# Zero matmuls planned into TensorE's gaps at the start of an attention and FFN kernel, with changes to an eviction's engine, a load step and the last stores

## The chip, the cores and the metric

The kernel runs on one core of a Trainium2 chip. The metric is the device time of one execution in microseconds; lower is better. Five engines share the work: TensorE (PE), VectorE (DVE), ScalarE (ACT), GpSimd (POOL) and SyncE (SP), which here only issues DMAs.

## The reference

Memory attention for 8 batches of 8 heads, then a feed-forward layer over the 4,608 tokens:

```python
a = softmax(phi, axis=2)                       # batch, head, token, 32 memories
k_m, v_m = a^T k, a^T v                        # per batch and head: 32 x 64
attn = softmax(q k_m^T / 8, axis=-1)           # token x 32
x = concat_heads(attn v_m)                     # 4608 x 512
h = x @ w_in                                   # 512 x 2048
g = h * erf(softplus(h))
out = g @ w_out                                # 2048 x 512
```

Inputs and output are float32; `w_in` and `w_out` arrive as float64 words and are decoded on the chip.

## The kernel before

**Work.** For one batch `memories` computes the memories' weights (exponential of phi), then `k_m` and `v_m` by the 40 small matmuls of `one_memory` (L504, called kvmv below), evicts them (`kvk`, L514 and L516), turns them with two transposes (L521) and writes `km` and `vm` (L534, L537). `attention` multiplies q by `km` (L547), and DVE and ACT make the softmax of it: transpose (L593), maximum, subtract, exponential on ACT (L601), sum, reciprocal, product (L607) and a transpose back into `at` (L614). `vw` multiplies `w_in` by `vm` (also L547), so that the first FFN product is `psh = vw x at` (`ffn1`, L645) and x is never formed.

**Steps.** A step is one of 16 blocks of 128 FFN columns of one batch; there are 128. Per step `ffn1` makes two halves of 288 tokens in PSUM, DVE copies each into `h` (L655), ACT makes softplus (L662, from `h` into `e`) and erf (L667), DVE multiplies `e` and `h` into `g` (L679 in the first batch, L686 later), and `ffn2` multiplies `g` by `w_out` into the accumulators `pso0` to `pso3` (L712), four column blocks a step, six steps after `ffn1` (`LAG`). The 64 tokens that remain per batch go two batches at a time into `psr`. In the first batch (steps 0 to 15) `ffn2` uses float32 operands, later pairs of float32r parts (`g_hi`, `g_lo`); `ffn1` changes to pairs at step 4. Softplus, erf and exponential need different ACT tables, so steps run in groups of four: four softplus, then four erf.

**Weights.** Each of the 8 blocks of `w_in` and of `w_out` is 1 MB. `decode` turns one into float32 with a clamp (L393), a merge (L407) and a sign instruction (L429) on DVE and two instructions on ACT (L399, L403).

**Order.** Class `Plan` records every operation with an engine, a cost in ns, a rank (100 per step, some ahead of or behind it), its reads and writes. `Plan.order` then builds the order by a simulation: at each turn, of what can start soonest on each engine, the operation with the lowest rank; the instructions are issued in just that order, and semaphores do the rest. Buffers count too: pool `raw` holds 4 tiles for phi, kv and q, `wo` 8 for weights, `ot` 2 for results, `el` 5 of `h` and 5 of `e`, `ps` 4 PSUM banks.

**Start and end.** 12 matmuls of zeros (`warm`, L326) open TensorE's work. The first loads are issued in a fixed order: phiT, phi, two kv, the first `w_in`, two kv, two q, then weights. The loads and the memory work of the second batch are entered 14 steps ahead of its first step (L814). At the end `store` (L750) evicts each accumulator with one ACT instruction of 128x512 into a tile of pool `ot` (L753), and SP sends it out (L755).

Of the kernel before, what the change touches and what calls it, by code (L numbers as in the profile page):

```python
# [42 lines left out]
class Op:  # L43
    def __init__(self, engine, cost, rank, emit, kind, nbytes, edge):
        self.engine, self.cost, self.rank, self.emit = engine, cost, rank, emit
        self.kind, self.nbytes, self.edge = kind, nbytes, edge
        self.before, self.after, self.tiles, self.placed = set(), [], set(), []
        self.ready = self.start = self.end = 0.0


class Plan:
# [6 lines left out]
    RELOAD = 100.0  # L58
    NEAR = 100.0

    def __init__(self, room, any_order):
# [9 lines left out]

    def op(self, engine, cost, rank, reads, writes, emit, kind=None, nbytes=0, edge=None, after=(), holds=()):
        x = Op(engine, cost, rank, emit, kind, nbytes, edge)
        x.before.update(after)
# [30 lines left out]
    def order(self):  # L105
# [10 lines left out]
        landed, warm_at, pe_end = 2200.0, 4000.0, 0.0  # L116
        releases, out, now, held = [], [], 0.0, set()

        def fits(x):
# [8 lines left out]
            return all(room[p] >= n for p, n in need.items())  # L128

        while len(out) < len(self.ops):  # L130
            best = None
            for e, xs in waiting.items():
                can = [x for x in xs if fits(x)]
                if e == ACT and not at_edge:
                    can = [x for x in can if x.kind != "exp"]
                if not can:
                    continue
                t0 = max(free[e], now, min(x.ready for x in can))
                can = [x for x in can if x.ready <= t0 + self.NEAR]
                if e == PE and small and any(x.kind == "small" and x.ready <= t0 for x in can):  # L140
                    can = [x for x in can if x.kind == "small" and x.ready <= t0]
                x = min(can, key=lambda x: x.rank)
                t = max(free[e], x.ready, now)
                if best is None or t < best[0]:
                    best = (t, x)
            if releases and (best is None or releases[0][0] <= best[0]):
# [3 lines left out]
            if best is None:  # L150
                raise RuntimeError(f"nothing fits after {len(out)} of {len(self.ops)}")
            now, x = best
            e = x.engine
            waiting[e].remove(x)
# [5 lines left out]
            cost, late = x.cost, 0.0  # L160
            if e == PE:
                if now - pe_end > 3400:
                    warm_at = now + 4000
                if now < warm_at:
                    cost *= 2
                if (x.kind == "small") != small:
                    small = not small
                    cost += self.SWITCH if small else self.SWITCH + self.RELOAD
                pe_end, late = now + cost, 170.0
            elif e == ACT:  # L170
                if x.kind is not None and x.kind != table:
                    cost += self.TABLE
                    table = x.kind
                if x.edge is not None:
                    at_edge = x.edge
                late = 75.0
            elif e == DVE:
                late = 60.0
            free[e] = now + cost
            x.start, x.end = now, now + cost + late  # L180
# [5 lines left out]
            for y in x.after:  # L186
                n_wait[y] -= 1
                y.ready = max(y.ready, x.end + self.SIGNAL)
                if not n_wait[y]:
                    waiting[y.engine].append(y)  # L190
            for k in x.tiles:
# [9 lines left out]
def tile_memory_attention_then_erf_softplus_ffn(  # L201
# [11 lines left out]
    P = 128  # L213
# [22 lines left out]
    FR1, FR2 = 4, 16  # L236
    WARM = (12, 12, 16)

# [82 lines left out]

    def warm(n, rank, after):
        def emit():
            t = pools["ps"].tile([P, DM], F32, name="warm", tag="ps")
            for _ in range(n):
                nc.tensor.matmul(out=t, lhsT=zeros[:, :P], rhs=zeros, start=True, stop=True)  # L326

        key = plan.tile("ps", "warm", n, rank)
        return op(PE, 216 * n, rank, [("zeros",)], [key], emit, after=after)

# [299 lines left out]
    def ffn1(rank, i, half):  # L630
# [10 lines left out]
        def emit():  # L641
# [74 lines left out]
    def ffn2(rank, i, d):  # L716
# [11 lines left out]

        op(PE, mm(DM, True) if exact else 3 * mm(DM, False), rank, gs + [w_key, o], [o], emit)
        if k == NK - 1:  # L730
# [19 lines left out]
    def store(rank, o, rows):  # L750
        t = tile_("ot", "ot", *o)
        op(ACT, on_act(DM, True), rank - 30, [o], [t],
           lambda: nc.scalar.activation(get(t), get(o), AF.Identity))  # L753
        for n, (r, ln) in enumerate(rows):
            op(SP, 60, rank, [t], [], lambda n=n, r=r, ln=ln: nc.sync.dma_start(  # L755
                out=out[r : r + ln], in_=get(t)[n * ln : (n + 1) * ln]), nbytes=ln * DM * 4)

# [12 lines left out]

    for g in range(NG):
        load_phiT(-2000, 0, g)
    load_phi(-1999, 0)
    load_kv(-1998, 0, 0)
    load_kv(-1997, 0, 1)
    load_weight(-1996, "in", 0)
    load_kv(-1995, 0, 2)
    load_kv(-1994, 0, 3, "wo")
    load_q(-1993, 0, "wo")
    load_q(-1992, 1, "wo")  # L780
    load_weight(-1991, "in", 1)
    load_weight(-1990, "out", 0)
    for c in range(2, NPR):
# [3 lines left out]

    w = [warm(WARM[0], -3000, ())]
    memories(at(-10), at(-9), 0)
# [10 lines left out]
    for c in range(NPR):  # L800
        if c:
            when(2 * c - 3, decode, at(2 * c - 3), "in", c)
            when(2 * c - 1, vw, at(2 * c - 1.5), 0, c, 1, 2 * c < FR1)
        when(2 * c, decode, at(second[2 * c] - 3.5), "out", c)
        n = second[16 + 2 * c] - 5 - c
        when(n, split_wo, at(n), c)
# [89 lines left out]
```

## Time and profile before

| | |
|---|---|
| median of 3 runs | 739.71 us (738.8 to 740.99) |
| the profiled execution's own time | 740.94 us |
| its span, first to last instruction | 739.2 us |
| TensorE busy | 710.2 us, 96% of the span |
| VectorE busy | 524.4 us, 71% |
| ScalarE busy | 446.5 us, 60% |
| GpSimd busy | 100.5 us, 14% |
| mean granted TensorE clock | 0.972 of full speed |

The busy share of an engine is an average over the span. In the strip of 40 slices (18.5 us each) TensorE shows 6, 5, 6 tenths in the first three, 9 or more from there to the last but one, and 6 in the last; its granted clock is 7, 5, 8 and 8 tenths in the first four slices and full after. DMA is at 9, 9, 9 and 6 tenths in the first four.

### The profile page before, as it was taken

How to read it: one execution, taken by the hardware profiler on the slowest of the kernel's cores; microseconds unless marked ns; L12 is line 12 of the kernel's file. 1: busy time of each engine (PE TensorE's matmuls, PEld its weight loads, DVE VectorE, ACT ScalarE, POOL GpSimd, SP SyncE). 2: the span in 40 equal slices, each digit the busy share in tenths (PEclk: the TensorE clock that was granted, in tenths of full speed). 3: DMA queues.
4: the chain of work that ended last, by engine and by line, in shares of the span. 5: the costliest groups of instructions: out<-in, count | busy, mean ns of one | idle time of the engine just before them, and what ended most of it. 6: DMA issues, size and time to landing. Idle time of an engine off the chain costs nothing.

```text
span 739.2 us, 12098 instructions
## 1 busy us (share of the span) xinstructions
PE 710.2 (96%) x4716; PEld 550.2 (74%) x4716; DVE 524.4 (71%) x975; ACT 446.5 (60%) x691; POOL 100.5 (14%) x246
## 2 busy tenths in 40 slices
PE   6569999999999999999999999999999999999996
PEld 3246555668788887888788887888878788888885
DVE  3898998879875687777755496777754587666730
ACT  4698887776776566585753457574654266454611
POOL 0001111110111011111111011111111111111110
PEclk7588999999999999999999999999999999999999
DMA  9996313162331224211130212311210100010002
GB/s 307 379 385 212 114 58 128 38 213 81 94 117 32 90 63 124 86 58 33 65 97 1 90 47 73 120 44 47 65 33 1 58 15 1 1 51 7 1 1 71
DMA packets 30392, 64.74 MB, mean 88 GB/s; under 512 B 2688, under 2 KB 13440, under 8 KB 29312
## 3 DMA queue, kind: packets, MB, share of 16 engines
q1 hardware_dynamic: 30336, 63.97, 26.0%
q8 instruction: 37, 0.61, 0.3%
q14 instruction: 19, 0.16, 0.1%
HBM read 54.53 MB, written 9.44 MB: 87 GB/s over the span
## 4 chain that ended last, share of the span: by engine, by line
PE 91%; DMA 6%; ACT 1%; SPq 1%; DVE 0%; issue 0%; ACTq 0%
PE pso L712 50%; PE psh L645 27%; PE psr L712 6%; PE psa L547 5%; DMA kv<-kv 2%; PE psa L504 2%; DMA phiT<-phiT 2%; DMA q<-qT 1%; DMA out<-ot 1%; PE psa L521 0%; ACT w L403 0%; SPq L346 0%; ACT ot L753 0%; SPq L359 0%; SPq L361 0%
## 5 line engine op out<-in xcount | busy, mean ns | idle before, releaser
L712 PE MATMUL pso<-wo,g_hi 128*128 128x512 f32 x896 | 281.1, 395 | 0.0
L662 ACT ACTIVATE e<-h 128x576 f32<-128x576 f32 x128 | 87.7, 685 | 176.0 <-DVE h L655 175.6
L712 PEld LDWEIGHTS pso<-wo,g_hi 128*128 128x128 f32 x896 | 159.9, 188 | 32.4 <-issue 6.8
L712 PE MATMUL pso<-wo,g_lo 128*128 128x512 f32 x448 | 176.0, 393 | 0.0
L655 DVE COPY h<-psh 128x288 f32<-128x288 f32 x256 | 114.7, 451 | 42.1 <-PE psh L645 40.1
L645 PE MATMUL psh<-at_hi,vw_hi 128*128 128x288 f32 x496 | 114.1, 311 | 0.0
L645 PEld LDWEIGHTS psh<-at_hi,vw_hi 128*128 128x128 f32 x496 | 84.6, 189 | 29.6 <-issue 8.6
L645 PE MATMUL psh<-at_lo,vw_hi 128*128 128x288 f32 x496 | 106.4, 296 | 0.0
L645 PE MATMUL psh<-at_hi,vw_lo 128*128 128x288 f32 x496 | 106.0, 295 | 0.0
L686 DVE TENSOR_TENSOR e<-e,h 128x576 f32<-128x576 f32 x112 | 82.9, 751 | 29.3 <-ACT e L667 29.2
L693 POOL CAST rest<-g_hi 128x64 fp32r<-128x64 f32 x112 | 50.5, 452 | 388.2 <-DVE g_hi L688 379.8
L712 PEld LDWEIGHTS pso<-wo,g_lo 128*128 128x128 f32 x448 | 84.1, 188 | 19.3
L688 DVE CAST g_hi<-e 128x576 fp32r<-128x576 f32 x112 | 50.9, 457 | 64.1 <-PE pso L712 52.1
L689 DVE TENSOR_TENSOR g_lo<-e,g_hi 128x576 fp32r<-128x576 f32 x112 | 86.3, 771 | 5.4 <-PE pso L712 0.6
L667 ACT ACTIVATE e<-e 128x576 f32<-128x576 f32 x128 | 80.6, 676 | 0.4
L645 PEld LDWEIGHTS psh<-at_hi,vw_lo 128*128 128x128 f32 x496 | 80.1, 189 | 0.0
L645 PEld LDWEIGHTS psh<-at_lo,vw_hi 128*128 128x128 f32 x496 | 79.3, 188 | 0.0
L712 PE MATMUL pso<-w,g 128*128 128x512 f32 x112 | 53.4, 612 | 0.0
L693 POOL CAST rest<-g_lo 128x64 fp32r<-128x64 f32 x112 | 36.6, 327 | 109.6 <-DVE g_lo L689 101.8
L712 PE MATMUL psr<-wo,rest 128*128 128x512 f32 x192 | 49.0, 390 | 0.0
L317 ACT ACTIVATE vw_hi<-psa 128x512 fp32r<-128x512 f32 (+1 forms) x68 | 35.3, 554 | 22.1 <-PE psa L547 22.0
L319 DVE TENSOR_TENSOR vw_lo<-psa,vw_hi 128x512 fp32r<-128x512 f32 (+1 forms) x68 | 41.7, 632 | 6.8 <-ACT vw_hi L317 6.7
(79 smaller groups left out, 692.1 us busy)
## 6 DMA issues: line engine op xcount, KB each, us to landing
kv<-kv SPq DMA_DIRECT2D x32, 512.0 KB, 5.0
q<-qT SPq DMA_DIRECT2D x16, 576.0 KB, 5.2
w<-w_in SPq DMA_DIRECT2D x8, 1024.0 KB, 11.1
w<-w_out SPq DMA_DIRECT2D x8, 1024.0 KB, 11.3
out<-ot SPq DMA_DIRECT2D x32, 256.0 KB, 2.1
phiT<-phiT SPq DMA_DIRECT2D x16, 288.0 KB, 3.1
phi<-phi SPq DMA_DIRECT2D x8, 512.0 KB, 5.7
kv<-kv SPq DMA_DIRECT2D x32, 64.0 KB, 4.9
```

The lines of the kernel that those rows point to most:

```text
L317: lambda: nc.scalar.activation(get_hi(), get_src(), AF.Identity))
L319: lambda: nc.vector.tensor_tensor(out=get_lo(), in0=get_src(), in1=get_hi().bitcast(F32), op=ALU.subtract))
L547: nc.tensor.matmul(out=get(ps[par])[p * M : (p + 1) * M, :], lhsT=w()[rows, p, :], rhs=x()[rows, p, :], start=True, stop=True,)
L645: nc.tensor.matmul(out=get(ps), lhsT=x[:, g, k % 4 * P : (k % 4 + 1) * P], rhs=y[:, g, :], start=(n + g == 0), stop=(n == len(parts) - 1 a ...
L655: op(DVE, on_dve(U), rank - 20, [ps], [(h, half)], lambda: nc.vector.tensor_copy(out=get(h)[:, half * U : (half + 1) * U], in_=get(ps)))
L662: last[:] = [op(ACT, on_act(S), rank, [("h", i)], [e], lambda: nc.scalar.activation(get(e), get(("h", i)), AF.Softplus), kind="softplus", ...
L667: last[:] = [op(ACT, on_act(S), rank, [e], [e], lambda: nc.scalar.activation(get(e), get(e), AF.Erf), kind="erf", edge=edge, after=last)]
L686: op(DVE, on_dve(S), rank, [e, h], [e], lambda: nc.vector.tensor_tensor(out=get(e), in0=get(e), in1=get(h), op=ALU.mult))
L688: op(DVE, on_dve(S, 1), rank, [e], [hi], lambda: nc.vector.tensor_copy(out=get(hi), in_=get(e)))
L689: op(DVE, on_dve(S), rank, [e, hi], [lo], lambda: nc.vector.tensor_tensor(out=get(lo), in0=get(e), in1=get(hi).bitcast(F32), op=ALU.subtract))
L693: lambda x=x, y=y: nc.gpsimd.tensor_copy(out=rest[:, k, x, cols], in_=get(y)[:, NT * P :]))
L712: nc.tensor.matmul(out=o, lhsT=y, rhs=z, start=(start and n == 0), stop=(stop and n == len(parts) - 1))
```

## The change

- `warm` is gone. Instead the planner notes a number `fill` for a TensorE operation that starts more than 450 ns after the one before it: gap less 200 ns, divided by 216 ns or, where the planner's picture of the clock is low, 432 ns. That many zero matmuls (128x512, bfloat16, into a bank of its own that later becomes `pso0`) are issued ahead of the operation. This ends with the first `ffn2` of a batch (kind "stop filling"). The groups, in order: 14, 12, 3, 15, 3, 2, 2, 35, 8, 11, 4, 3, in all 112, where before there were 12.
- The copy of `psh` into `h` may go to DVE or ACT for steps 0 to 15, whichever the planner finds free sooner. In the built program ACT has 17 of these 32, DVE 15.
- The second batch's loads and memory work are entered 12 steps ahead (`o - 12`) instead of 14.
- `store`: for the last batch and its `psr`, the tile comes from tag `h` (5 buffers) instead of `ot` (2), and the eviction is two instructions of 256 columns, one on ACT, one on DVE.
- Without effect on the built program: `AHEAD` is 0, so the new branch that uses it is never taken; the first loads are written as a list in the same order; the other value for `split_wo` applies at `2 * c >= 16`, which does not occur.

```diff
+class Clock:
[...]
...
-        waiting = {e: [x for x in self.ops if x.engine == e and not n_wait[x]] for e in ENGINES}
+        waiting = {e: [x for x in self.ops if e in x.ways and not n_wait[x]] for e in ENGINES}
...
+        def best_way(x):
+            return min(x.ways, key=lambda e: max(free[e], x.ready, now) + x.ways[e][0])
...
             if e == PE:
-                if now - pe_end > 3400:
-                    warm_at = now + 4000
-                if now < warm_at:
-                    cost *= 2
+                filling = filling and x.kind != "stop filling"
+                gap = now - max(free[PE], 1100.0)
+                if filling and gap > 450:
+                    x.fill = int((gap - 200) / (216 if clock.fast else 432))
+                    clock.to(now, 1.0)
+                else:
+                    clock.to(now, 0.0)
...
+                if not clock.fast:
+                    cost *= 2
...
-    WARM = (12, 12, 16)
+    H_EITHER = 16
...
+    def fill(n):
+        if n and not idle:
+            idle.append(pools["po"].tile([P, DM], F32, name="idle", tag="pso0"))
+        for _ in range(n):
+            nc.tensor.matmul(out=idle[0], lhsT=zeros[:, :P], rhs=zeros, start=True, stop=True)
...
-        op(DVE, on_dve(U), rank - 20, [ps], [(h, half)], lambda: nc.vector.tensor_copy(
-            out=get(h)[:, half * U : (half + 1) * U], in_=get(ps)))
+        op(DVE, on_dve(U), rank - 20, [ps], [(h, half)],
+           lambda: nc.vector.tensor_copy(out=keep(), in_=get(ps)),
+           other={ACT: (on_act(U, True), lambda: nc.scalar.activation(keep(), get(ps), AF.Identity))}
+           if i < H_EITHER else ())
...
-        t = tile_("ot", "ot", *o)
-        op(ACT, on_act(DM, True), rank - 30, [o], [t],
-           lambda: nc.scalar.activation(get(t), get(o), AF.Identity))
+        final = o[1] >= B - 2 if o[0] == "psr" else o[1] == B - 1
+        t = tile_("h" if final else "ot", "ot", *o)
+        halves = [(0, DM // 2, ACT), (DM // 2, DM, DVE)] if final else [(0, DM, ACT)]
...
-        n = o - 14 if b == 1 else max(o - 21, NK - 2)
+        n = o - 12 if b == 1 else max(o - 21, NK - 2)
...
+        fill(x.fill)
         x.emit()
```

The planner's new costs move instructions on every engine in the first batch. Three places follow.

**VectorE, the last rows up to the first product `g`** (`h` copies, `at_lo` and `vw_lo` are float32r remainders, `pmx`, `psm`, `prs`, `phi` belong to the second batch's memory, `w` rows are decodes). Before:

```order
L407 SCALAR_TENSOR_TENSOR w<-w 128x1024
L393 TENSOR_SCALAR w<-w 128x1024
L487 TENSOR_SCALAR psm<-psm 128x1
L429 SCALAR_TENSOR_TENSOR w<-w 128x1024
L487 TENSOR_SCALAR psm<-psm 128x1
L489 RECIPROCAL prs<-psm 128x1 x2
L655 COPY h<-psh 128x288 x2
L393 TENSOR_SCALAR w<-w 128x1024
L407 SCALAR_TENSOR_TENSOR w<-w 128x1024
L393 TENSOR_SCALAR w<-w 128x1024
L429 SCALAR_TENSOR_TENSOR w_in_104<-w 128x4x256
L679 TENSOR_TENSOR g<-e,h 128x576
```

Now:

```order
L443 SCALAR_TENSOR_TENSOR w<-w 128x1024
L356 TENSOR_TENSOR vw_lo<-psa,vw_hi 128x256
L465 SCALAR_TENSOR_TENSOR w<-w 128x1024
L356 TENSOR_TENSOR vw_lo<-psa,vw_hi 128x256
L443 SCALAR_TENSOR_TENSOR w<-w 128x1024
L696 COPY h<-psh 128x288
L465 SCALAR_TENSOR_TENSOR w_in_104<-w 128x4x256
L493 TENSOR_SCALAR pmx<-pmx 128x1 x2
L429 TENSOR_SCALAR w<-w 128x1024
L721 TENSOR_TENSOR g<-e,h 128x576
```

Between the transposes into `at` and the first `g` stand, now as before, 4 merges, 4 sign instructions, two `at_lo`, two `vw_lo` and two maxima; gone from there are 6 of 10 `h` copies, 1 of 5 clamps, and the second memory's `phi` (two instructions), `psm` and `prs` (two each). On ACT the four erf of steps 0 to 3 now stand ahead of the second memory's exponentials, not behind them.

**TensorE, around the first `ffn2`.** Before:

```order
L504 MATMUL psa<-kv,phi 32x128 x20
L547 MATMUL psa<-w_in_104,vm_101 32x256 x8
L645 MATMUL psh<-at_hi,vw_hi 128x288 x2
L645 MATMUL psh<-at_lo,vw_hi 128x288 x2
L645 MATMUL psh<-at_hi,vw_lo 128x288 x2
L712 MATMUL pso<-w,g 128x512 x3
```

Now (the fill row is the last of three; ahead of the three stands `psa<-w_in_104,vm_101`):

```order
L365 MATMUL idle<-zeros 128x512
L501 MATMUL psa<-ident,bias 128x128 x2
L681 MATMUL psh<-at_hi,vw_hi 128x288 x2
L681 MATMUL psh<-at_lo,vw_hi 128x288 x2
L681 MATMUL psh<-at_hi,vw_lo 128x288 x2
L754 MATMUL pso<-w,g 128x512 x2
L681 MATMUL psh<-at_hi,vw_hi 128x288 x2
L681 MATMUL psh<-at_lo,vw_hi 128x288 x2
L681 MATMUL psh<-at_hi,vw_lo 128x288 x2
L754 MATMUL pso<-w,g 128x512 x2
L540 MATMUL psa<-kv,phi 32x128 x20
```

The second batch's first kvmv (20 rows here, 40 in the trace, where a float32 matmul is two) stood ahead of the first `ffn2` and now stands behind its four.

**TensorE, the third batch's second kvmv and its first q product** (`psa<-q,km_99`). Before:

```order
L504 MATMUL psa<-kv,phi 32x128 x20
L712 MATMUL pso<-wf,g 128x512 x2
L521 MATMUL psa<-ident,kvk 128x128 x2
L645 MATMUL psh<-at_hi,vw_hi 128x288 x2
L645 MATMUL psh<-at_lo,vw_hi 128x288 x2
L645 MATMUL psh<-at_hi,vw_lo 128x288 x2
L645 MATMUL psh<-at_hi,vw_hi 128x288 x2
L645 MATMUL psh<-at_lo,vw_hi 128x288 x2
L645 MATMUL psh<-at_hi,vw_lo 128x288 x2
L547 MATMUL psa<-q,km_99 32x288 x8
```

Now, the last rows ahead of that product; the kvmv stands eight rows further up, with two `ffn1` halves and the transposes between:

```order
L754 MATMUL pso<-w,g 128x512 x4
L681 MATMUL psh<-at_hi,vw_hi 128x288 x2
L681 MATMUL psh<-at_lo,vw_hi 128x288 x2
L681 MATMUL psh<-at_hi,vw_lo 128x288 x2
L681 MATMUL psh<-at_hi,vw_hi 128x288 x2
L681 MATMUL psh<-at_lo,vw_hi 128x288 x2
L681 MATMUL psh<-at_hi,vw_lo 128x288 x2
L754 MATMUL pso<-wf,g 128x512 x4
L583 MATMUL psa<-w_in_105,vm_102 32x512 x8
L583 MATMUL psa<-q,km_99 32x288 x8
```

On SP the rows agree up to the fourth `w_in` load; after it two of the second batch's kv loads stand ahead of the next `w_out`. GpSimd's rows change place with the products they copy from.

## Rows read from the trace of the kernel before

**Rows 1.** Windows, TensorE alone: length, busy us (instructions), granted clock, DMA share, GB/s.

```profile
0.00:9.00 9.00, 5.36 (x14) 1.00 0.81 275
9.00:37.00 28.00, 17.15 (x158) 0.51 1.04 366
37.00:49.00 12.00, 8.62 (x54) 1.00 1.03 374
49.00:61.00 12.00, 9.13 (x69) 0.57 1.04 381
61.00:732.00 671.00, 669.30 (x4423) 1.00 0.20 63
```

**Rows 2.** Timeline of the first 61 us, TensorE: start, us, what, idle before and releaser.

```profile
16.82 2.50 PE L504 MATMUL psa<-kv,phi 128*32 128x128 f32 x36 [1.18 <-DMA kv<-kv]
19.87 0.76 PE L521 MATMUL psa<-ident,kvk 128*128 128x128 f32 x2 [0.55 <-ACT kvk L514]
20.57 2.85 PE L547 MATMUL psa<-q,km 64*32 64x288 f32 x32
31.54 4.18 PE L645 MATMUL psh<-at,vw_hi 128*128 128x288 f32 x8 [7.04 <-DVE at L614]
56.91 4.38 PE L712 MATMUL pso<-w,g 128*128 128x512 f32 x6
61.92 0.42 PE L645 MATMUL psh<-at_hi,vw_hi 128*128 128x288 f32 x2
```

**Rows 3.** The same timeline, the weight loads of two neighbouring zero matmuls.

```profile
1.59 0.15 PEld L326 LDWEIGHTS <-zeros 128*128 128x128 bf16 x1 [0.27 <-issue]
2.02 0.15 PEld L326 LDWEIGHTS <-zeros 128*128 128x128 bf16 x1 [0.28 <-issue]
```

**Rows 4.** Timeline after 61 us, TensorE: the same work at the higher clock.

```profile
63.51 0.38 PE L521 MATMUL psa<-ident,kvk 128*128 128x128 f32 x2
64.69 1.43 PE L504 MATMUL psa<-kv,phi 128*32 128x128 f32 x40
67.04 0.66 PE L547 MATMUL psa<-w_in,vm 64*32 64x256 f32 x16
73.85 0.72 PE L547 MATMUL psa<-q,km 64*32 64x288 f32 x16
127.08 1.88 PE L712 MATMUL pso<-w,g 128*128 128x512 f32 x4
```

**Rows 5.** Chain of waits in order of time: start, us, engine, tile, line.

```profile
80.57 3.43 PE pso L712 x8
159.66 1.58 PE psh L645 x12
```

**Rows 6.** Timeline, VectorE: start and end of its first chain, and two later products.

```profile
22.50 1.81 DVE L593 STREAM_TRANSPOSE sc<-psa 128x288 f32<-128x288 f32 x4 [2.95 <-PE psa L547]
30.62 1.43 DVE L614 STREAM_TRANSPOSE at<-sc 128x576 f32<-128x576 f32 x2
54.03 0.75 DVE L679 TENSOR_TENSOR g<-e,h 128x576 f32<-128x576 f32 x1
124.08 1.42 DVE L679 TENSOR_TENSOR g<-e,h 128x576 f32<-128x576 f32 x2
```

**Rows 7.** Groups of instructions, shapes apart: count, busy us, mean ns, idle before.

```profile
L655 DVE COPY h<-psh 128x288 f32<-128x288 f32 x256 | 114.7, 451 | 42.1 <-PE psh L645 40.1
L393 DVE TENSOR_SCALAR w<-w 128x1024 f32<-128x1024 f32 x16 | 11.0, 685 | 4.4 <-DMA w<-w_in 4.4
L572 ACT ACTIVATE vw_hi<-psa 128x256 f32<-128x256 f32 x4 | 1.3, 382 | 2.2 <-PE psa L547 2.2
```

**Rows 8.** Windows, all engines: length, PE, PEld, DVE, ACT, POOL busy, clock, DMA share, GB/s.

```profile
65.00:70.00 5.00, 5.00 (x70) 3.35 (x62) 5.00 (x9) 4.96 (x12) 0.00 (x0) 1.00 0.58 182
100.00:140.00 40.00, 40.00 (x216) 23.70 (x201) 36.55 (x63) 28.32 (x41) 5.50 (x7) 1.00 0.19 60
```

**Rows 9.** Timeline, ScalarE: the second memory's exponentials, first and last instruction.

```profile
45.85 1.28 ACT L485 ACT_TABLE_LOAD   x1
49.63 0.40 ACT L480 ACTIVATE phi<-phi 64x256 f32<-64x256 f32 x1
```

**Rows 10.** Timeline, third batch's first q product: its load and the product.

```profile
151.85 0.93 SPq L376 DMA_DIRECT2D q<-qT  x2
157.24 0.84 PE L547 MATMUL psa<-q,km 64*32 64x288 f32 x16 [1.70 <-DMA q<-qT]
```

**Rows 11.** Timeline of the end: last matmuls and evictions.

```profile
731.14 1.52 PE L712 MATMUL psr<-wo,rest 128*128 128x512 f32 x6
732.04 1.28 ACT L753 ACTIVATE ot<-pso 128x512 f32<-128x512 f32 x2 [1.48 <-DMA out<-ot]
734.82 0.60 ACT L753 ACTIVATE ot<-psr 128x512 f32<-128x512 f32 x1 [1.49 <-DMA out<-ot]
```

More of the change, by code (lines that the diff above doesn't have):

```diff
@@ L70, in tile, with op @@
         return key
-    def op(self, engine, cost, rank, reads, writes, emit, kind=None, nbytes=0, edge=None, after=(), holds=()):
-        x = Op(engine, cost, rank, emit, kind, nbytes, edge)
+    def op(self, engine, cost, rank, reads, writes, emit, kind=None, nbytes=0, edge=None, after=(),
+           holds=(), other=()):
+        x = Op({engine: (cost, emit), **dict(other)}, rank, kind, nbytes, edge)
         x.before.update(after)
@@ L135, in order @@
                     can = [x for x in can if x.kind != "exp"]
+                can = [x for x in can if len(x.ways) == 1 or best_way(x) == e]
                 if not can:
@@ L138, in order @@
                 t0 = max(free[e], now, min(x.ready for x in can))
[L139 to L142, printed above, removed]
+                near = [x for x in can if x.ready <= t0 + self.NEAR]
+                if e == PE and small and any(x.kind == "small" and x.ready <= t0 for x in near):
+                    near = [x for x in near if x.kind == "small" and x.ready <= t0]
+                elif e in (ACT, DVE) and self.AHEAD:
+                    near = [x for x in can if x.ready <= t0 + self.AHEAD]
+                    near = [min(near, key=lambda x: x.rank + self.WORTH * max(0.0, x.ready - t0))]
+                x = min(near, key=lambda x: x.rank)
                 t = max(free[e], x.ready, now)
                 if best is None or t < best[0]:
-                    best = (t, x)
+                    best = (t, x, e)
             if releases and (best is None or releases[0][0] <= best[0]):
@@ L151, in order @@
                 raise RuntimeError(f"nothing fits after {len(out)} of {len(self.ops)}")
-            now, x = best
-            e = x.engine
-            waiting[e].remove(x)
+            now, x, e = best
+            x.engine, (cost, x.emit) = e, x.ways[e]
+            for w in x.ways:
+                waiting[w].remove(x)
             for k in x.placed:
@@ L168, in order @@
                     cost += self.SWITCH if small else self.SWITCH + self.RELOAD
-                pe_end, late = now + cost, 170.0
+                if not clock.fast:
+                    cost *= 2
+                clock.to(now + cost, Clock.SMALL if x.kind == "small" else 1.0)
+                late = 170.0
             elif e == ACT:
@@ L189, in order @@
                 if not n_wait[y]:
-                    waiting[y.engine].append(y)
+                    for w in y.ways:
+                        waiting[w].append(y)
             for k in x.tiles:
@@ L320, in split @@
                out=get_lo(), in0=get_src(), in1=get_hi().bitcast(F32), op=ALU.subtract))
[L322 to L329, printed above, removed]
+    idle = []
+    def fill(n):
[3 more added lines that the diff above has]
+            nc.tensor.matmul(out=idle[0], lhsT=zeros[:, :P], rhs=zeros, start=True, stop=True)
     def load(rank, key, nbytes, emit):
@@ L769, in tile_memory_attention_then_erf_softplus_ffn @@
             second[k] = k + (3 if near else LAG)
[L771 to L782, printed above, removed]
+    FIRST = ["phiT0", "phiT1", "phi", "kv0", "kv1", "in0", "kv2", "kv3", "q0", "q1", "in1", "out0"]
+    for n, name in enumerate(FIRST):
+        x, rank = int(name[-1]) if name[-1].isdigit() else 0, n - 2000
+        if name[:-1] == "phiT":
+            load_phiT(rank, 0, x)
+        elif name == "phi":
+            load_phi(rank, 0)
+        elif name[:-1] == "kv":
+            load_kv(rank, 0, x, "raw" if x < 3 else "wo")
+        elif name[:-1] == "q":
+            load_q(rank, x, "wo")
+        else:
+            load_weight(rank, name[:-1], x)
     for c in range(2, NPR):
```

41 lines of the change are left out of this document (32 added, 9 removed).

## The prediction

> **What bounds the kernel now.** I read the windows of TensorE first, because its busy share is 96% and an average hides where the rest is. From 61 to 732 us it is busy 669.30 of 671 us at the full clock [rows 1]: there the time is the sum of its matmuls, and nothing on another engine counts unless it makes TensorE wait. Everything it loses lies at the two ends. Up to 61 us the windows hold 40.3 us of busy time, part of it at half speed: the granted clock is 0.51 (1.2 GHz of 2.4) from 9 to 37 us and 0.57 from 49 to 61 us [rows 1]. So the second view is TensorE's timeline of the head, and for each of its waits who ended it: a kv load at 16.82, ACT's `kvk` at 19.87, DVE's `at` at 31.54 [rows 2]. The third view is VectorE: its first chain starts when the q products arrive, at 22.50, ends its transposes at 32.05, and the first `g` starts at 54.03 [rows 6]. Between those two it works without a pause worth naming, so the number of its instructions ahead of the first `g` sets when `ffn2` can start, which it does at 56.91 [rows 2]. Last, the end: the last matmul ends at 732.66, but the last eviction only at 735.42, because it waited 1.49 us for a transfer to free its tile [rows 11]. I look for what moves the first `ffn2`, what the clock costs around it, later waits of TensorE, and the tail.
>
> **The change part by part.** The sum is made against the profiled execution's own 740.94 us; the median of the runs shown is 1.23 us lower, and I take that off at the end.
>
> *Clock up to the q products.* The zero matmuls keep TensorE busy between the first small products. The second kvmv still starts at 16.82, since it waits for a load whose place in SP's order is unchanged. At the higher clock its 36 instructions take 36/40 of 1.43, so 1.29 instead of 2.50 [rows 2, 4], 1.2 less; the two transposes 0.38 instead of 0.76, 0.4 less; the first 16 q products, which VectorE waits for, 0.72 instead of half of 2.85, 0.7 less. That is 2.3 us. Groups of 3 and 2 zero matmuls stand between them. A zero matmul takes 0.43 us at the low clock [rows 3], so by halving some 0.21 at the high one (an estimate), and the groups take 1.1 us, of which 0.5 lies in the gap that ACT leaves anyway [rows 2]. I take 1.6 us; the ends are 0 and 2.3.
>
> *VectorE's work ahead of the first `g`.* From there go 6 `h` copies of 0.451, a clamp of 0.685 [rows 7], and the second memory's `phi` and sums. These six I price by the nearest rows as two copies' worth for the large one and half a `h` copy for each of the others, 2 x 0.45 + 5 x 0.23 = 2.0. In all 2.7 + 0.7 + 2.0 = 5.4 us. The first `g` then starts at 54.03 - 1.6 - 5.4 = 47.0. I add 1 us because the fourth `w_in` block's decode now comes earlier and the DMA engines are full until 61 us [rows 1]: 48.0, end 48.8. TensorE's own order adds to it: three VectorE rows ahead of that `g` stands the sign instruction that releases a group of `vw` products; behind them come 3 zero matmuls, two transposes and half an `ffn1` before the first `ffn2`, 0.66 + 0.65 + 0.38 + 0.80 = 2.5 us [rows 4, 5]. The sign ends 0.9 us ahead of the `g`, at 47.1, so the first `ffn2` starts near 49.7, where it was 56.91: **7.2 us earlier**. The ends are 8.1 (as soon as `g` is there) and 3 (only half of the two parts comes through).
>
> *Clock around the first `ffn2`.* From 56.91 to 61.92 TensorE runs 6 `ffn2` and one half of `ffn1`, 5.01 us [rows 2]. At the high clock that is 6 x 0.43 + 0.80 = 3.4 us [rows 5]. **1.6 us less**, if the clock is still up then; the ends are 0 and 1.6.
>
> *Second memory two steps later.* Its first kvmv was hidden ahead of the first `ffn2` and now follows it: **1.4 us more** [rows 4]. It waits for ACT's exponentials, a stage from 45.85 to 50.03 before [rows 9] that now follows the fourth erf; TensorE has 4.2 us of work (four `ffn2`, one half) until it gets there, so I add **0.3**, with ends 0 and 2. Two ACT table loads stay two.
>
> *The third batch's q product.* It waited 1.70 us for its load, issued at 151.85 when the kvmv ahead of it freed the tile [rows 10]. Now TensorE has two halves, the transposes, four `ffn2`, two halves, four `ffn2` and a `vw` between: over 11 us, against the 5.4 us from issue to use. **1.7 us less**; no reason leaves part of it.
>
> *The end.* The last eviction waits for no transfer (5 tiles, not 2) and each engine copies half: 0.38 on ACT (256 columns), at most 0.45 on DVE [rows 7]. It can end at 732.66 + 0.1 + 0.45 = 733.2 instead of 735.42 [rows 11]: **2.2 us less**. Ends: 1.5, if the two SP issues of the last rows queue behind the four before them, and 2.4.
>
> *What costs nothing, and its cover.* The first 51 zero matmuls and the 35 ahead of `ffn1` run while TensorE would wait: for the kv load (1.18), for `kvk` (0.55), for `at` (7.04) [rows 2]. The 35 take 7.5 us from the end of the `vw` products, which I put at 22.6, so until 30.1, and the first `at` comes at 31.35 - 1.6 = 29.8; if the cover is short, a group delays what follows by its excess, 0.2 to 0.5 us here. They come from TensorE alone and touch no queue of SP or POOL.
>
> *`h` copies on ACT.* 17 copies of 0.38 are 6.5 us more for ACT, 7.7 less for VectorE [rows 7]. ACT is full (4.96 of 5.00) at 65 us, and from 100 to 140 us VectorE has 36.55 of 40, ACT 28.32 [rows 8]. TensorE wants every `g` 7 us sooner. The thinnest place before is the thirteenth `g`, ready at 124.8 [rows 6] and first used halfway through the four matmuls from 127.08, at 128.0 [rows 4]: 3 us. I take **1.0 us** of new waits between 55 and 140 us, ends 0 and 5.
>
> The sum: -7.2 - 1.6 + 1.4 + 0.3 - 1.7 - 2.2 + 1.0 = -10.0, so 730.9 for an execution like the profiled one, and **729.7** against the median.
>
> A rule speaks against counting on the clock. The Trainium skill (TensorE: Matmul & The Clock Gate, "What's actually happening") says the warm-up costs below 1% of a typical kernel's span and should not be fitted to a count of cold matmuls. By that the two clock terms of 1.6 us would be worth nothing, and the sum would come to 732.9. The rows of 49 to 61 us show a second cold stretch in the middle of dense work, which is why I keep them; of rival 2's chance, 0.03 is for the skill's reading.
>
> **The rivals.**
> 1. *ACT and VectorE can't feed TensorE* (0.20). The head ends earlier, but between 60 and 140 us TensorE waits for `g`. For it: ACT's 4.96 of 5. Against it: VectorE loses 7.7 us of copies. Price: 4 us of waits in place of 1.0, so 732.7.
> 2. *The head is not shortened* (0.11). ACT's order or the loads hold the first `g` where it was, less the clock's 1.6, since the DMA share is 1.04 up to 61 us [rows 1]. Then -1.6 - 1.6 + 1.4 - 1.7 - 2.2 = -5.7 and 1 us of waits for zero matmuls that were planned too long: 736.2 - 1.2 = 735.0.
> 3. *Slower: the clock stays low while the zero matmuls run* (0.05). Their number is fixed, so at 0.43 us each they push real work back. The 12 at the start are still 0.43 apart two microseconds in [rows 3]. If all 44 ahead of the second kvmv run so, TensorE reaches it near 1.2 + 44 x 0.43 + 4.3 of small work = 24.4 instead of 16.8, 7.6 us late, and the 42 up to `ffn1` add 9.0; with the 3.2 us of clock terms lost as well, -10.0 + 7.6 + 9.0 + 3.2 gives about 749.5. It decides when some 10 us are lost so, which takes the low clock into the group of 35. The Trainium skill (same page and section) says that the number of cold matmuls changes from run to run. By that rule single runs could differ by a few us.
>
> My forecast has 0.60; 0.04 is left for what I don't see.
>
> **How the numbers follow.** The forecast's own range is 726.5 to 732.5 (bounds of the first `ffn2` and of the new waits). With rivals 1 and 2 it reaches to 736. I give **726.5 to 736**. A measurement can tell 0.3%, 2.2 us, so faster means below 737.5: the forecast, rival 1 and nearly all of rival 2, 0.91. Within 0.3%: 0.05. Slower: 0.04.
>
> **What would show it.** Right: granted clock 1.00 from about 10 to 61 us; the first `at` transposes near 29; the first `ffn2` near 49.7 and 0.43 us for each of its matmuls; no 1.70 wait at the third batch's q; last eviction within 0.7 us of the last matmul. Wrong: zero matmuls 0.43 apart behind the first 14; TensorE's waits between 55 and 140 us above 2 us, released by ACT or DVE; a first `ffn2` after 53.

## The result, and the profile after

The changed kernel takes **730.95 us** (median of 4 runs, 729.75 to 733.4); the kernel before, on the same chip, 740.01 (4 runs). The ratio is 0.9883, 95% interval 0.9851 to 0.9914: faster by 1.2%, which is 8.7 us by the ratio and 9.1 by the two medians. Forecast were 729.7 us and a range of 726.5 to 736.

The profiled execution is the fastest of the four (729.75 us). I ran the same kernel again later (first experiment below), and its second profiled execution is an ordinary one (731.80 us). Cut at three points that every profile shows, the spans are:

| us | before | after | after, second profile |
|---|---|---|---|
| start to first `ffn2` | 56.91 | 48.76 | 50.81 |
| from there to the end of the last matmul | 675.75 | 674.57 | 674.59 |
| to the end of the last eviction | 2.76 | 0.88 | 0.88 |
| to the end of the span | 3.78 | 3.79 | 3.72 |
| span | 739.2 | 728.0 | 730.0 |

Most comes from the first line, 8.15 of 11.2 us in the first profile and 6.10 of 9.2 in the second; about 1.2 us come from the second line (the middle stretch, below) and 1.9 from the third. The two executions of the changed kernel differ by 2.05 us in the first line and by 0.07 or less in the others.

Windows of the changed kernel, TensorE alone (columns as in [rows 1]):

```profile
9.00:37.00 28.00, 27.57 (x240) 1.00 1.05 382
37.00:49.00 12.00, 11.44 (x84) 1.00 1.02 381
49.00:61.00 12.00, 12.00 (x86) 1.00 0.97 355
```

The granted clock is 1.00 where it was 0.51 and 0.57. The busy time up to 49 us now holds zero matmuls too, so it says nothing about progress; for that one reads where named products stand. TensorE's timeline of the head, to be read against [rows 2]:

```profile
12.10 3.40 PE L365 MATMUL idle<-zeros 128*128 128x512 bf16 x15
15.43 1.97 PE L540 MATMUL psa<-kv,phi 128*32 128x128 f32 x40
18.93 0.97 PE L583 MATMUL psa<-q,km 64*32 64x288 f32 x16
20.19 0.84 PE L583 MATMUL psa<-q,km 64*32 64x288 f32 x16 [0.29 <-DMA q<-qT]
29.66 4.04 PE L681 MATMUL psh<-at,vw_hi 128*128 128x288 f32 x16
46.27 0.67 PE L583 MATMUL psa<-w_in,vm 64*32 64x256 f32 x16 [0.55 <-DVE pmx L493]
48.76 1.88 PE L754 MATMUL pso<-w,g 128*128 128x512 f32 x4
53.08 1.43 PE L540 MATMUL psa<-kv,phi 128*32 128x128 f32 x40
```

Fifteen zero matmuls take 3.40 us, 0.22 each. The 7.04 us wait for `at` is filled; the first four `ffn2` matmuls take 1.88 us, the time at the full clock [rows 4]; and the second memory's product, now behind them at 53.08, waits for nothing.

VectorE, against [rows 6]: the first chain starts 2.56 us sooner, `at` 2.36, the first `g` 7.24.

```profile
19.94 0.85 DVE L629 STREAM_TRANSPOSE sc<-psa 128x288 f32<-128x288 f32 x2 [2.21 <-PE psa L583]
28.26 1.43 DVE L650 STREAM_TRANSPOSE at<-sc 128x576 f32<-128x576 f32 x2
46.79 0.74 DVE L721 TENSOR_TENSOR g<-e,h 128x576 f32<-128x576 f32 x1
```

Behind the head TensorE waits three times, 1.18 us in all; the 1.70 us wait for the third batch's q [rows 10] is gone:

```profile
78.82 0.73 PE L681 MATMUL psh<-at_hi,vw_lo 128*128 128x288 f32 x2 [0.28 <-DVE vw_lo L356]
83.97 0.67 PE L583 MATMUL psa<-w_in,vm 64*32 64x256 f32 x16 [0.32 <-DVE w_in L465]
129.16 1.42 PE L540 MATMUL psa<-kv,phi 128*32 128x128 f32 x36 [0.58 <-DMA kv<-kv]
```

And the end, against [rows 11]:

```profile
721.81 1.52 PE L754 MATMUL psr<-wo,rest 128*128 128x512 f32 x6
723.37 0.42 DVE L803 COPY ot<-psr 128x256 f32<-128x256 f32 x1 [0.94 <-PE psr L754]
723.83 0.38 ACT L800 ACTIVATE ot<-psr 128x256 f32<-128x256 f32 x1 [0.98 <-DVE ot L803]
```

No eviction waits for a transfer any more. But the halves don't run side by side: ACT's starts when VectorE's has ended, and VectorE is its releaser. Together they take 0.84 us, where one whole copy took 0.60. The four `pso` ahead of this one go the same way. The Trainium skill has a reason (PSUM — Partial Sum Buffer, "PSUM bank collisions raise a hardware error"): two engines may not touch the same 32-partition quadrant of one PSUM bank at once, disjoint columns included, and semaphores are to guard PSUM by bank and quadrant. The trace agrees with such a guard, 0.04 us between the halves of all five. Both halves also write one `ot` tile; no run here tells which of the two makes them take turns, or what would happen without the guard.

### The profile page after: what moved, and what is told of

It is laid out like the page before. It is cut to its first block, busy times and chain, and to the rows that moved or that the text cites. A ratio compares the mean times of both kernels' runs of the same rounds, so it can differ in the third digit from the quotient of the medians.

```text
span 728.0 us, 12307 instructions
## 1 busy us (share of the span) xinstructions
PE 720.0 (99%) x4816; PEld 553.8 (76%) x4816; DVE 521.0 (72%) x963; ACT 449.9 (62%) x708; POOL 98.7 (14%) x246
## 4 chain that ended last, share of the span: by engine, by line
PE 87%; DMA 6%; ACT 4%; DVE 1%; SPq 1%; issue 1%
PE pso L754 48%; PE psh L681 26%; PE psr L754 6%; PE psa L583 5%; DMA w<-w_in 4%; PE psa L540 2%; DMA kv<-kv 2%; ACT w L439 1%; ACT w L435 1%; ACT e L709 0%; ACT L709 0%; PE psa L557 0%; ACT e L704 0%; DVE w L443 0%; ACT vw_hi L354 0%
## 5 line engine op out<-in xcount | busy, mean ns | idle before, releaser
L696 DVE COPY h<-psh 128x288 f32<-128x288 f32 x239 | 107.8, 452 | 42.8 <-PE psh L681 41.2
## 6 DMA issues: line engine op xcount, KB each, us to landing
w<-w_out SPq DMA_DIRECT2D x8, 1024.0 KB, 11.2
```

The lines of the kernel that those rows point to most:

```text
L696: lambda: nc.vector.tensor_copy(out=keep(), in_=get(ps)),
```

## The experiments

Twelve kernels ran, in three groups of four on three chips, each group beside the kernel before (its medians: 740.25, 740.34, 740.07). All are the changed kernel with one edit, except where said. The theory (S) is the sum on record. Its rivals: the order alone did it (O), or the clock alone (Z).

| kernel | median us (runs) | ratio to before, 95% |
|---|---|---|
| the changed kernel again | 731.49 (4) | 0.9883 (0.987 to 0.9897) |
| no zero matmuls | 735.18 (5) | 0.9932 (0.992 to 0.9944) |
| none after the group of 35 | 732.88 (4) | 0.9896 (0.9881 to 0.9911) |
| none up to the group of 35 | 733.23 (4) | 0.9904 (0.9889 to 0.9919) |
| zero matmuls alone | 736.18 (6) | 0.9951 (0.9938 to 0.9964) |
| h copies on VectorE | 735.84 (5) | 0.994 (0.9927 to 0.9952) |
| second memory as before | 732.57 (5) | 0.99 (0.9885 to 0.9915) |
| store as before | 733.56 (5) | 0.9917 (0.9905 to 0.9929) |
| whole evictions | 731.88 (4) | 0.9888 (0.9875 to 0.99) |
| kv ahead of w_in | 734.77 (6) | 0.9935 (0.9913 to 0.9958) |
| transposes behind the half | 732.12 (4) | 0.9887 (0.9871 to 0.9904) |
| transposes behind the first ffn2 | 731.56 (4) | 0.9881 (0.9867 to 0.9896) |

Below, differences are taken to 731.49, the changed kernel's second median, unless said.

### The changed kernel again

No edit.

> The changed kernel itself once more, for more of its runs and a second profiled one: its four runs lie 3.6 us apart (729.75 to 733.4), the kernel before's eleven 1.6 us. Theory L (the loads): the time from the first ffn2 to the last matmul is 674.6 us (674.57 in the profile of the changed kernel, 674.73 with whole evictions) in every execution, and what varies is when the loads of kv and q let the second kvmv and the q products start: a profiled run near 731 to 733 has its first ffn2 2 us or so after 48.76, with waits of TensorE for kv. Rival W (waits later on): the first ffn2 stands near 48.8 again and the difference lies between 55 and 140 us.

Measured: 731.36 to 731.8. Theory L holds for the two profiles: the middle stretch is 674.59 us against 674.57, and the first `ffn2` stands 2.05 us later. Timelines of TensorE and VectorE:

```profile
17.02 1.42 PE L540 MATMUL psa<-kv,phi 128*32 128x128 f32 x36 [0.23 <-DMA kv<-kv]
21.44 0.84 PE L583 MATMUL psa<-q,km 64*32 64x288 f32 x16 [0.50 <-DMA q<-qT]
50.81 1.88 PE L754 MATMUL pso<-w,g 128*128 128x512 f32 x4
...
29.51 1.43 DVE L650 STREAM_TRANSPOSE at<-sc 128x576 f32<-128x576 f32 x2
40.23 0.70 DVE L429 TENSOR_SCALAR w<-w 128x1024 f32<-128x1024 f32 x1 [1.19 <-DMA w<-w_in]
```

Where it starts is SP's own issue of the loads. The last kv row and the q loads, SP's timeline, in the first profile of the changed kernel:

```profile
7.53 0.47 SPq L397 DMA_DIRECT2D kv<-kv  x1
8.04 1.54 SPq L412 DMA_DIRECT2D q<-qT  x2
```

and in the second:

```profile
8.63 0.47 SPq L397 DMA_DIRECT2D kv<-kv  x1
9.14 1.81 SPq L412 DMA_DIRECT2D q<-qT  x2
```

SP goes on 1.10 us later though no releaser is named. In the profile of before it issued that row at 8.54, and in the eleven others with this order of loads between 8.63 and 9.40: the first profile after, with 7.53, was the lucky one. At `at` the second profile is 1.25 us behind the first; from there the lateness grows by a later wait of VectorE for `w_in` (1.19 us against 0.38).

### The zero matmuls: none, none late, none early, and they alone

```diff
-        fill(x.fill)
+        fill(0)
```

> The changed kernel with all 112 zero matmuls left out; the order of everything else is kept. Theory S (the sum on record): the zero matmuls are worth the two clock terms, 1.6 us up to the q products and 1.6 us around the first ffn2, so 3.2 us more than the changed kernel, 734 us (733 to 736), with the first ffn2 near 50.4 (48.76 with them) and a granted clock near 0.5 from 9 to 37 us. Rival O (the order does it all): the reordered head alone shortens the time and the zero matmuls only fill waits, 731 us, first ffn2 within 0.5 us of 48.76. Rival Z (the clock does it all): without the zero matmuls nearly the whole gain of the head is gone, 738 us or more, first ffn2 after 54.

Measured: 3.7 us more. The first `ffn2` moves from 50.81 to 52.88, 2.07 us, and the middle stretch grows from 674.59 to 676.28, 1.69 us (the last matmul ends at 729.16). The two clock terms of the sum were 1.6 and 1.6. The cut at the first `ffn2` lies inside the second slow stretch: up to `at` 1.39 us are lost (29.51 to 30.90), and 2.06 from the last `vw` product ahead of the first `ffn2` to the second memory's product behind it. O (no loss) and Z (7 us) fall. TensorE's timeline:

```profile
17.10 2.50 PE L540 MATMUL psa<-kv,phi 128*32 128x128 f32 x36 [1.03 <-DMA kv<-kv]
31.82 5.98 PE L681 MATMUL psh<-at,vw_hi 128*128 128x288 f32 x16 [7.03 <-DVE at L650]
52.88 3.47 PE L754 MATMUL pso<-w,g 128*128 128x512 f32 x4
```

The 36 products take 2.50 us again instead of 1.42, and the first four `ffn2` 3.47 instead of 1.88.

The two other cuts divide the groups at the one of 35:

```diff
+    late = False
     for x in plan.order():
         begin = len(traced)
-        fill(x.fill)
+        fill(x.fill if not late else 0)
+        late = late or x.fill > 20
```

(this one drops the last 26; the other has `if late` and drops the first 86).

> The changed kernel without the last four groups of zero matmuls (8, 11, 4 and 3, all between 35 and 50 us); the 86 ahead of them stay, and so does the order. Theory S: these groups hold the clock around the first ffn2 alone, so the second clock term, 1.6 us, is lost (and 0.65 us for the last three may come back): 1 to 1.6 us over the changed kernel's 731.5, so 732.5 to 733.1, with a granted clock below 0.8 from 49 to 61 us. Rival E (only the early zero matmuls matter): 731.5 or less.

> The changed kernel without its first 86 zero matmuls (all up to and including the group of 35); the 26 behind them stay. Theory S: the small products up to q, and the first exact ffn1, run at the low clock, while the stretch around the first ffn2 runs at the high one: the first clock term, 1.6 us, and up to 0.5 us for the exact ffn1: 1.6 to 2.1 us over the changed kernel's 731.5, so 733.1 to 733.6, first ffn2 near 52.5. Without any zero matmul the loss was 3.7 us; if the two parts add, b3 and b4 together lose as much. Rival E: the whole 3.7 us are lost here, 735.2.

Measured: 1.4 and 1.7 us more, by the ratios 1.0 and 1.6; rival E is out for the early cut (735.2 by it); for the late cut (731.5 or less) the medians speak against it, while the ratios' intervals overlap. Windows without the late groups, then without the early ones:

```profile
9.00:37.00 28.00, 25.52 (x230) 1.00 1.04 364
49.00:61.00 12.00, 11.64 (x89) 0.86 0.99 376
```

```profile
9.00:37.00 28.00, 16.92 (x148) 0.88 1.05 369
49.00:61.00 12.00, 11.81 (x100) 1.00 0.99 371
```

Without the late groups TensorE waits four times between 36 and 50 us, 5.3 us in all, and the clock falls just ahead of the first `ffn2`; I had expected a clock below 0.8, it was 0.86. Where each loss stands is read from rows:

| us | the changed kernel again | none | none after 35 | none up to 35 |
|---|---|---|---|---|
| start to `at` | 29.51 | 30.90 | 30.67 | 30.79 |
| last `vw` product ahead of the first `ffn2` to the second memory's product | 6.83 | 8.89 | 7.76 | 6.81 |

Without the early groups 1.28 us are lost up to `at`, though the second kvmv's 36 products start no later (16.99 against 17.02), and nothing around the first `ffn2`. Without the late groups 0.93 us are lost around the first `ffn2`. That profile's `at` is 1.16 us late for another reason, the loads: its q products wait 0.23 and 0.93 us for q. TensorE:

```profile
22.60 0.84 PE L583 MATMUL psa<-q,km 64*32 64x288 f32 x16 [0.93 <-DMA q<-qT]
```

So both terms exist, each in its place, but the 1.4 us of the late half may hold a share of the loads'. Together the two lose 3.1 us, where dropping all lost 3.7. By ratios it is 2.5 against 3.6, and each ratio is uncertain by 0.9 us or more, so whether the parts add exactly stays open.

Last, the zero matmuls without the rest of the change:

```diff
-    H_EITHER = 16
+    H_EITHER = 0
...
-        final = o[1] >= B - 2 if o[0] == "psr" else o[1] == B - 1
+        final = False
...
-        n = o - 12 if b == 1 else max(o - 21, NK - 2)
+        n = o - 14 if b == 1 else max(o - 21, NK - 2)
```

> Planned zero matmuls in the head as in the changed kernel, but the h copies of the first batch on VectorE alone, the second memory and its loads two steps earlier as before, and evictions of the last rows whole on ACT into the old tiles; the planner orders it afresh. Theory S: the clock terms of 1.6 and 1.6 us remain, the end's 2.2 and the VectorE work taken from ahead of the first g (5.4 us) do not, the 1.7 us wait at the third batch's q comes back, the second memory's 1.7 is not paid: 740.0 - 3.2 = 737 us (735 to 738), first g near 52. Rival O: within 0.5 us of the kernel before, 740. Rival Z: 733 or less.

Measured: 4.1 us below before's 740.25, 3.6 by the ratio; the sum gave 3.2. O and Z fall here too. One row of the surplus is plain: in the planner's fresh order the third batch's q product waits 0.59 us where it waited 1.70 [rows 10], 1.1 us less. It isn't the only difference. In the profiled execution, the fastest of the six, the first `ffn2` comes 4.12 us earlier than before, 1.64 of it at `at`; the rest is the fresh order's too, so this run doesn't price the clock alone. VectorE, then TensorE:

```profile
51.48 0.75 DVE L721 TENSOR_TENSOR g<-e,h 128x576 f32<-128x576 f32 x1
...
151.00 0.84 PE L583 MATMUL psa<-q,km 64*32 64x288 f32 x16 [0.59 <-DMA q<-qT]
```

### The h copies

```diff
-        x.emit()
+        (x.ways[DVE][1] if len(x.ways) > 1 else x.emit)()
```

> The changed kernel, its order kept, with the 17 h copies that ACT took put back on VectorE (0.451 us each, 7.7 us in all, 6 of them ahead of the first g). Theory S: the first g comes 6 x 0.45 = 2.7 us later, TensorE's start of ffn2 with it, and the later 11 copies cost up to 1 us of waits: 2.7 to 4 us over the changed kernel, 734 to 735. Rival F (VectorE had slack, the order of the loads and the planner did it): less than 1 us.

Measured: 4.35 us more, above the upper end of 4. The split was wrong too. VectorE, then TensorE:

```profile
30.15 1.43 DVE L650 STREAM_TRANSPOSE at<-sc 128x576 f32<-128x576 f32 x2
40.53 0.70 DVE L429 TENSOR_SCALAR w<-w 128x1024 f32<-128x1024 f32 x1
50.26 0.75 DVE L721 TENSOR_TENSOR g<-e,h 128x576 f32<-128x576 f32 x1
...
88.44 0.67 PE L583 MATMUL psa<-w_in,vm 64*32 64x256 f32 x16 [0.98 <-DVE w_in L465]
122.34 0.53 PE L681 MATMUL psh<-at_lo,vw_hi 128*128 128x288 f32 x2 [0.45 <-DVE at_lo L356]
```

The first `g` comes 1.40 us later (48.86 to 50.26), and 0.64 of that is `at`, late by its loads. So the six copies ahead of it cost 0.76 us, not 2.7: they fill VectorE's 1.19 us wait for `w_in`, which is gone from the row at 40.53, and one of 0.23 for `psh`; and though a copy's row reads 0.45, VectorE's next row starts some 0.37 us after it, so six hold it 2.2. The larger part comes later. Between 61 and 136 us the named waits sum to 2.69 us (0.60, 0.98, 0.13, 0.45, 0.53), where the changed kernel has 1.25. In all 3.9 us separate the two profiles: 1.15 at the first `ffn2`, 1.44 in these waits, and 1.2 in the middle stretch between rows that read as busy, for which I have no releaser.

### The second memory

```diff
-        n = o - 12 if b == 1 else max(o - 21, NK - 2)
+        n = o - 14 if b == 1 else max(o - 21, NK - 2)
```

> The changed kernel with the second memory and its loads two steps earlier, as before; the planner orders it afresh. Theory S: moving the memory back takes 1.4 us of kvmv from behind the first ffn2 to ahead of it and 0.3 of its wait, but brings its phi and sums (2.0 us) back ahead of the first g on VectorE; the first ffn2 comes 2 us later or more: within 1 us of the changed kernel, 731 to 732.5. The 1.7 us wait at the third batch's q does not hang on this edit. Rival M: the later memory carries the gain, 734 or more.

Measured: 1.1 us more, 732.57, 0.07 above S's range; M is out. VectorE's first `g` moves back, the first `ffn2` with it:

```profile
51.74 0.76 DVE L721 TENSOR_TENSOR g<-e,h 128x576 f32<-128x576 f32 x1 [0.54 <-ACT e L709]
...
55.57 3.60 PE L754 MATMUL pso<-w,g 128*128 128x512 f32 x8
```

The first `ffn2` is 4.8 us later for a loss of 1.1, because TensorE did the kvmv and several halves of `ffn1` ahead of it: with another order, the place of the first `ffn2` is no measure. The q wait is absent here as well, so its going doesn't hang on this edit.

### The end

```diff
-        halves = [(0, DM // 2, ACT), (DM // 2, DM, DVE)] if final else [(0, DM, ACT)]
+        halves = [(0, DM, ACT)]
```

> The changed kernel with each eviction of the last rows whole on ACT, still into the tiles of tag h. In the changed kernel's profile the two halves of the last tile run one after the other, VectorE 723.37 to 723.79 and ACT 723.83 to 724.21. If that is a wait of one for the other, a whole copy (0.60 us in the profile before) ends 0.2 to 0.3 us sooner after the last matmul and the time is unchanged, 731 (730 to 731.5). If the halves do bring the end's gain, the last eviction ends later after the last matmul than the 0.88 us of the changed kernel, and the time is 1 us longer or more.

```profile
724.36 1.52 PE L754 MATMUL psr<-wo,rest 128*128 128x512 f32 x6
725.92 0.60 ACT L800 ACTIVATE ot<-psr 128x512 f32<-128x512 f32 x1 [0.76 <-PE psr L754]
```

The last eviction ends 0.64 us after the last matmul instead of 0.88: the halves cost 0.24 us. The median, 731.88, doesn't show it (0.4 us more, within the intervals; in this profile the kv loads came late, TensorE waited 2.1 us for them). What brings the end's gain is the tile:

```diff
-        final = o[1] >= B - 2 if o[0] == "psr" else o[1] == B - 1
+        final = False
```

> The changed kernel with the evictions of the last rows as before: whole, on ACT, into the two tiles of tag ot. Theory S: the last eviction waits again for a transfer that frees its tile and ends about 2.8 us after the last matmul (2.76 in the profile before, 0.88 in the changed one), so 1.9 to 2.2 us more than the changed kernel, 733 us. If the tail is not on the path that sets the time, 731.

```profile
724.64 1.52 PE L754 MATMUL psr<-wo,rest 128*128 128x512 f32 x6
728.31 0.60 ACT L800 ACTIVATE ot<-psr 128x512 f32<-128x512 f32 x1 [1.49 <-DMA out<-ot]
```

Measured: 2.1 us more, 2.5 by the ratio. The wait of 1.49 for a transfer is back, the eviction ends 2.75 us after the last matmul. The kernel with whole evictions differs from this one in the tile alone: 0.64 against 2.75, 2.1 us.

### Three attempts to go on

The loads set the head, so I moved the first `w_in` block behind the kv loads (with whole evictions):

```diff
-    FIRST = ["phiT0", "phiT1", "phi", "kv0", "kv1", "in0", "kv2", "kv3", "q0", "q1", "in1", "out0"]
+    FIRST = ["phiT0", "phiT1", "phi", "kv0", "kv1", "kv2", "kv3", "in0", "q0", "q1", "in1", "out0"]
```

> The changed kernel with whole evictions of the last rows on ACT, and the first w_in block (1 MB, issued between the second and the third kv load) issued behind the fourth kv load; the planner orders it afresh. Theory L: at the 360 GB/s of the head the block takes 2.8 us, by which the second pair of kv loads lands sooner; the q loads do not, so the q products start at most 1 to 2 us sooner, and VectorE's decode of the block moves from its idle time into the stretch ahead of the first g: 0 to 2 us less than the changed kernel, 729 to 731. Rival V (VectorE's work ahead of the first g decides): the decode costs as much as the loads gain or more, 731 to 733.

Measured: 3.3 us more, runs 733.1 to 738.25; beyond both theories, V the nearer.

```profile
15.15 1.42 PE L540 MATMUL psa<-kv,phi 128*32 128x128 f32 x36 [0.44 <-DMA kv<-kv]
27.60 0.66 PE L583 MATMUL psa<-w_in,vm 64*32 64x256 f32 x16
77.18 1.57 PE L540 MATMUL psa<-kv,phi 128*32 128x128 f32 x40 [1.83 <-DVE h L696]
```

The second kvmv comes 1.9 us sooner, but the `w_in` product stands at 27.60 instead of 22.74, the first `g` at 50.47, and the new order has a wait of 1.83 us for an `h` copy, which neither theory had. The profiled execution is 1.0 us below the median; for the two runs near 738 there is no profile, and what made them late stays open.

Second, in the second profile the first `g` ends at 49.60 but `ffn2` starts at 50.81, behind three zero matmuls and the second memory's transposes. I moved those transposes (`turn`, and its first sum on VectorE, `add`) in the list, with whole evictions:

```diff
...
+    turn.fill = 0
+    n = seq.index([x for x in seq if x.kind == "stop filling"][0])
+    seq[n:n] = [turn, add]
```

> The changed kernel with whole evictions on ACT at the end (0.25 us sooner by the profiles), and with the second memory's two transposes moved from ahead of the first ffn2's half of ffn1 to behind it; the three zero matmuls that filled the wait for their bias are left out. In the second profile of the changed kernel the first g is ready at 49.60, but TensorE starts ffn2 only at 50.81, behind those zero matmuls (48.93) and the transposes (49.58, which wait for a bias that ends at 49.80). Now the half runs first, 48.93 to 49.9, then the transposes, and ffn2 starts near 50.3: 0.5 us, and 0.25 at the end, 730.7 (730.3 to 731.2). If VectorE or ACT hold what follows, only the 0.25 is left: 731.2 or more.

and one operation further (`+ 1`):

> As the kernel with the transposes behind the half of ffn1, but they go behind the first of the four matmuls of the first ffn2, which then starts near 49.9 instead of 50.81: 0.9 us, and 0.25 at the end, 730.3 (730 to 731). Against it: VectorE's sum with the transposes' result, which it starts at 50.79, waits 0.4 us longer, and its copies and the third g behind it; if that decides, 730.7 or more, no better than the other place.

Measured: 732.12 and 731.56, no gain. The second, TensorE:

```profile
49.35 1.02 PE L754 MATMUL pso<-w,g 128*128 128x512 f32 x2
52.32 0.51 PE L681 MATMUL psh<-at_hi,vw_hi 128*128 128x288 f32 x2 [0.87 <-DVE phi L511]
```

`ffn2` does start 1.46 us earlier than in the second profile (0.47 of it because the first `g` is that much earlier here), but the next half of `ffn1` now waits 0.87 us for VectorE's sum, and from the first `ffn2` to the last matmul it takes 1.24 us more. I had expected that wait at VectorE's copies and the third `g`; it came on TensorE itself. The first has the same wait, 0.54 us. None of the eleven edits beats the changed kernel.

## Why the prediction was right

The sum said -10.0 us for an execution like the one profiled. The two profiles after give -11.2 and -9.2. Term by term, in the order of the prediction:

- **First `ffn2`, -7.2.** Measured -8.15 and -6.10. Its start, the q products, was taken to be set by the clock alone (1.6 us); in the ordinary execution the q load is then the next bound (0.50 us of wait), and `at` comes 1.1 us earlier, not 1.6. The piece for VectorE's work was right in its net only: from `at` to the first `g` I forecast 4.4 us less, and it is 4.9 and 4.1. But the six copies are worth 0.76 us where they stand, not 2.7, since the wait for the fourth `w_in` block takes up most of it. I had booked that wait as 1 us by itself; it is 0.38 and 1.19. The second memory's rows, priced at 2.0, make that stretch 2.9 us longer when they are put back in a fresh order (0.54 of it a wait for ACT's erf). That the errors offset each other is luck. TensorE's own order was read rightly: 2.5 us from the last `vw` product ahead of it to `ffn2`, measured 2.49 and 2.48.
- **The clock, 1.6 and 1.6.** Measured 2.07 and 1.69 by leaving the zero matmuls out, cut at the first `ffn2`; by the rows of the two slow stretches 1.4 and 2.1. Dropping one half costs 1.3 us in those rows for the early groups and 0.9 for the late ones, 1.7 and 1.4 by the medians. The Trainium skill's reading (TensorE: Matmul & The Clock Gate, "What's actually happening"), that the warm-up costs below 1% of a span and isn't to be fitted to a count of cold matmuls, holds in its first half: 3.7 us are 0.5% of this span. But they are 40% of what this change gained; the sum without them, 732.9, is 1.4 to 2 us above the two medians. The parts don't add up to the whole: taken out one at a time, the zero matmuls, the copies, the memory's place and the end cost 11.2 us together, where the change gained 8.9.
- **Second memory, +1.4 and +0.3.** The kvmv stands behind the first `ffn2`, 1.43 us; the wait of 0.3 didn't come. Put back as before it costs 1.1 us net, where the terms together (2.0 of VectorE's work against 1.7) gave 0.3.
- **Third batch's q, -1.7.** The wait is gone in both profiles. That doesn't hang on the memory's place; a fresh order without the other edits has 0.59 left of the wait.
- **The end, -2.2.** Measured -1.88. The step that failed is "each engine copies half": they take turns, and the last eviction ends 0.88 us after the last matmul, outside the 0.7 that I had named as a sign. The tile alone would have given 2.1.
- **New waits, +1.0.** Measured 1.18 and 1.25, with their releasers VectorE and a kv load.

Of the rivals, the first (ACT and VectorE can't feed TensorE) would have needed 4 us of such waits; with the copies back on VectorE there are 2.69, more than twice the 1.25 with the change, but still less than 4. The second wanted the first `g` where it was but for the clock's 1.6 us; it came 5.2 us earlier or more. The third wanted zero matmuls 0.43 us apart in the group of 35; they are 0.22 apart (7.73 us for 35).

The forecast median is 1.2 to 1.8 us below the two medians measured. Of the 1.8, 0.9 is the sum's (730.9 against 731.8 for the second profiled execution). The first term is 1.1 short there, and 0.5 of that is the load of q, for which I took nothing; the other terms give some back. The other 0.9 is the last step, from the profiled execution to the median: I took off 1.23, but the second profiled execution lies 0.3 us above its median. An execution with late or early loads can be either.

## What to carry to other kernels

Where the main stretch is full, cut the span at two or three points that stay (the first main product, the last matmul, the last eviction) and predict each piece: differences between executions and between edits then have a place, and a median that hides a quarter of a microsecond can be left to the rows. Instructions taken from an engine can be worth less than their time when the engine then waits for a load, as the six copies were: look for that wait ahead of counting copies. And a copy split over two engines was no faster here, where both read one PSUM tile and write one result tile: measure the tile's release, not the copy.

## What the runs showed of the hardware

The granted clock read 1.00 in a stretch where products took the time of the lower level. Windows of the kernel without zero matmuls:

```profile
12.00:17.00 5.00, 2.51 (x22) 1.00 1.05 344
17.00:21.00 4.00, 3.35 (x42) 1.00 1.07 371
31.00:34.00 3.00, 2.18 (x5) 0.50 1.04 354
```

It reads 1.00 from 12 to 21 us, though the 36 products at 17.10 take 2.50 us, as in the kernel before at a granted 0.50 (1.42 at 1.00 with the zero matmuls). The mean of 0.88 from 9 to 37 us, where I had expected 0.5, is this. Here the durations of a known product tell the level; the column alone doesn't.

I had also not expected how much of the spread is the first loads': the same issue of the last kv row came between 7.53 and 9.40 us in thirteen profiles, and the runs of the changed kernel lie 3.6 us apart, with a middle stretch that agrees within 0.02 us in its two profiles.
